# A fused sliding-window attention and feed-forward kernel: w_in in a tile per load, x laid out by token block, attention of chunk 1 two blocks ahead, idle products during the first loads

## The chip, the cores and the metric

The kernel runs on one core of a Trainium2 chip. The metric is the device time of one execution in microseconds (us), from inputs in the chip's HBM to the output there; lower is better. It is compared by the median of several runs. Engines are named as in the profile: PE is TensorE, PEld its weight loads, DVE is VectorE, ACT ScalarE, POOL GpSimd, SP SyncE; SPq, ACTq and POOLq are the queues on which these engines issue DMAs.

## The reference

```python
# q, k, v: (8, 8, 576, 64) float32;  w_in: (512, 2048);  w_out: (2048, 512)
scores = scale * np.matmul(q, k.transpose(0, 1, 3, 2))      # scale = 1/8
rel = pos[:, None] - pos[None, :]
scores = np.where((rel >= 0) & (rel < 64), scores, -1e9)
attn = softmax(scores)
attn_out = np.matmul(attn, v)
x = attn_out.transpose(0, 2, 1, 3).reshape(8 * 576, 8 * 64)
h = x @ w_in
g = h * (1.0 / (1.0 + np.exp(-1.702 * h)))
return g @ w_out                                            # (4608, 512) float32
```

## The kernel before

The 4608 tokens are 36 blocks `m` of 128 tokens and 9 chunks `ch` of 512. A block holds two query groups of 64 tokens; a batch has nine such groups, so a block can lie in two batches.

**Attention of a block** is a chain over four engines. `scores(m)` makes sixteen small products on PE into the one PSUM tile `S`; `exp(m)` reads it on ACT into `E`; `mask(m)` multiplies by a 0/1 mask on DVE into `PT`; `pv(m)` makes sixteen products with v (which carries a column of ones for the row sums) into the one PSUM tile `Tacc`; `norm(m)` divides on DVE (`rc`, `xs`). The block is then turned into `xT`, [512 features in 4 groups of 128, tokens]: for chunks 0 to 3 by `x_mm` on PE and the copy `x_out` on ACT, for later chunks by a transposing DMA from SP (`x_dma`).

**q and k** must be turned as well (`qkt`). Batches 0 and 1 come in three parts of pairs (`load_pairs` on SP, `cast_pairs` to bf16 on two engines, `turn_pairs`: sixteen transposes on PE, and a copy each on DVE and ACT). Batch 2 comes by `load_qk` on SP, `cast_qk` on POOL, `turn_dma` on SP; batches 3 to 7 by casting loads on POOL (`load_bf16`) and `turn_dma`. `cast_v` and `shift_v` run on POOL.

**The feed-forward part**: `up_mm` multiplies w_in by xT (a unit is 16 products of 128 columns for one block, or 4 of 512 columns for a chunk) into `hps`, `up_th` (ACT, tanh) and `up_g` (DVE) make `gT`; `down` multiplies by w_out over 16 steps per chunk into `ops`; `down_out` scales on ACT or DVE and stores. From chunk 2 on, one unit of `up` of chunk ch and one step of `down` of chunk ch-1 make a slot (16 per chunk, the first is slot 32), and tables (`at`, `later`, `slot_pv`) say at which slot attention and loads are issued.

**What sets the order.** Each engine works through its instructions in the order in which the code issues them, and the code writes that order out by hand. Waits between engines are put in by the framework from what each instruction reads and writes of a tile. In the kernel before, w_in is one tile that three loads fill (512, 512 and 1024 of the 2048 columns, issued from POOL behind `gate`, a copy that waits for the last of the first k loads). The rows of xT are [4 feature groups, 512 tokens], so a block is four pieces of a row.

Of the kernel before, what the change touches and what calls it, by code (L numbers as in the profile page):

```python
# [29 lines left out]
def kernel(  # L30
# [94 lines left out]

    def cast_pairs(b, i, engines):
        n = pairs(i)
        for w in range(2):
            copy_on(
                engines[w],  # L130
                out=rows[b % 2][w][0:n, 2 * i : 2 * i + 2, :].rearrange(
                    "p r (h d) -> p h r d", d=D
                ),
                in_=stage_qk[(3 * b + i) % 2][0:n, w, :].rearrange(
                    "p (h r d) -> p h r d", r=2, d=D
                ),
            )

    def turn_pairs(b, i, tiles):
        n = pairs(i)  # L140
        for w in range(2):
            for r in range(2):
                for hp in range(4):
                    nc.tensor.transpose(  # L144
                        out=tiles[w][:, hp, r, 0:n],
                        in_=rows[b % 2][w][0:n, 2 * i + r, P * hp : P * hp + P],
                        identity=ident[0:n, 0:n],
                    )
        for w in range(2):
            copy_on(  # L150
                DA[w],
                out=qkt[b % 2][:, w::2, PAD + 256 * i : PAD + 256 * i + 2 * n].rearrange(
                    "p g (n r) -> p g n r", r=2
                ),
                in_=tiles[w][:, :, :, 0:n].rearrange("p g r n -> p g n r"),
            )
# [267 lines left out]
    norm(1)  # L424
    warm(2)
    x_mm(1, psO, "O")
    scores(2)
    exp(2)
    x_out(1)
    scores(3)  # L430
    exp(3)
# [187 lines left out]
```

## Time and profile before

| | |
|---|---|
| median of 3 runs | 333.69 us (332.8 to 335.26) |
| the profiled execution's own time | 335.44 us |
| its span, first to last instruction | 333.7 us |
| PE busy | 304.0 us (91% of the span), 3226 products |
| PE weight loads busy | 194.9 us (58%) |
| DVE, ACT, POOL busy | 164.6, 156.2 and 136.5 us |
| mean granted clock of PE | 0.984 |

The span is cut by the code into a head (first loads, attention of blocks 0 to 3, `up` of chunk 0, to 44.2 us), `down` of chunk 0 (to 61.2), a stage in which chunk 1's `up` and the attention of blocks 5 to 8 alternate (to 90.9), and the slots. A PE that is busy in the record is not at its peak, so what matters is where it stands idle, who ended each wait, and at which clock it ran.

### The profile page before, as it was taken

Reading aid. Unit: us, or ns where it says so; the run is one execution under the profiler, and the core shown is the slowest. Engines: PE = TensorE matmul, PEld = TensorE weight load, DVE = VectorE, ACT = ScalarE, POOL = GpSimd, SP = SyncE. Lnnn points to the kernel's source line nnn. Section 1 sums busy time; section 2 is a strip of 40 time slices with the busy share of each in tenths; the row PEclk is TensorE's granted clock in tenths of the full one; section 3 lists DMA queues with packets and bytes.
Section 4 is the critical chain, followed back from the end, with each engine's and each line's share of the span. In section 5 each row is a group of like instructions: output and inputs, shape, how many; then the busy total and the mean of one; then the engine's idle time right before and its main releaser. Section 6 shows DMA issues by size and latency. Waiting matters only on the chain.

```text
span 333.7 us, 7775 instructions
## 1 busy us (share of the span) xinstructions
PE 304.0 (91%) x3226; PEld 194.9 (58%) x3226; DVE 164.6 (49%) x276; ACT 156.2 (47%) x240; POOL 136.5 (41%) x196
## 2 busy tenths in 40 slices
PE   1677999778899979999899999999999999999995
PEld 1437545567767757777577777775555544444442
DVE  5352732467655535655455655555545554433400
ACT  2542622655555535564455454555455543444411
POOL 1850465086697869737876537720000000000000
PEclk9995999999999979999999999999999999999999
DMA  8999890599799999999999999994433312000121
GB/s 193 210 210 215 217 256 10 167 215 171 148 96 120 134 155 154 125 160 134 200 141 186 207 109 168 141 117 89 87 82 79 81 47 79 33 31 31 34 94 63
DMA packets 150995, 43.31 MB, mean 130 GB/s; under 512 B 135088, under 2 KB 145328, under 8 KB 150960
## 3 DMA queue, kind: packets, MB, share of 16 engines
q0 software_dynamic: 72480, 13.05, 56.1%
q1 hardware_dynamic: 74448, 22.43, 37.5%
q10 hardware_dynamic: 4032, 7.34, 6.8%
q8 instruction: 25, 0.41, 0.6%
q14 instruction: 10, 0.08, 0.1%
HBM read 36.70 MB, written 9.44 MB: 138 GB/s over the span
## 4 chain that ended last, share of the span: by engine, by line
PE 79%; DMA 9%; ACT 4%; DVE 2%; SPq 2%; POOL 1%; issue 1%; ACTq 0%
PE hps L336 36%; PE ops L366 36%; PE Tacc L280 4%; DMA w_in_sb<-in_moe_w_in_dram 3%; PE S L251 3%; DMA xT_dma<-xs 2%; DMA qkt<-rows_k 2%; DMA stage_qk<-in_k_dram 2%; ACT th L347 2%; ACT xT_pe L319 1%; DVE PT L266 1%; PE turn L144 1%; SPq L85 1%; ACT E L261 1%; SPq L119 1%
## 5 line engine op out<-in xcount | busy, mean ns | idle before, releaser
L353 DVE SCALAR_TENSOR_TENSOR gT<-th,hps 128x512 bf16<-128x512 bf16 x144 | 99.0, 688 | 121.5 <-ACT th L347 121.0
L366 PE MATMUL ops<-w_out_sb,gT 128*128 128x512 bf16 x576 | 144.6, 382 | 0.5 <-DVE gT L353 0.5
L347 ACT ACTIVATE th<-hps 128x512 bf16<-128x512 f32 x144 | 86.0, 597 | 123.7 <-PE hps L336 119.0
L336 PEld LDWEIGHTS <-w_in_sb 128*128 128x128 bf16 x1328 | 109.0, 115 | 47.3 <-issue 6.7
L336 PE MATMUL hps<-xT_dma,w_in_sb 128*128 128x256 bf16 (+1 forms) x448 | 82.5, 318 | 1.4 <-DMA xT_dma<-xs 1.4
L366 PEld LDWEIGHTS <-gT 128*128 128x128 bf16 x576 | 53.0, 98 | 52.5 <-issue 1.4
L336 PE MATMUL hps<-xT_pe,w_in_sb 128*128 128x128 bf16 (+1 forms) x880 | 67.6, 234 | 4.9 <-DMA w_in_sb<-in_moe_w_in_dram 2.6
L261 ACT ACTIVATE E<-S 128x1024 bf16<-128x1024 f32 x36 | 36.7, 1019 | 5.0 <-PE S L251 5.0
L172 POOL DMA_DIRECT2D v_nat<-in_v_dram x25 | 21.4, 854 | 17.5 <-issue 17.3
L380 ACT ACTIVATE o_sb<-ops 128x512 f32<-128x512 f32 x34 | 20.2, 599 | 17.5 <-PE ops L366 17.5
L293 DVE TENSOR_TENSOR xs<-Tacc,rc 128x512 bf16<-128x512 f32 x36 | 24.9, 692 | 1.2
L176 POOL COPY v_off<-v_nat 64x528 bf16<-64x528 bf16 x25 | 16.0, 642 | 18.2 <-DMA v_nat<-in_v_dram 17.5
L266 DVE TENSOR_TENSOR PT<-E,mask_None 128x1024 bf16<-128x1024 bf16 x28 | 21.0, 749 | 2.9 <-ACT E L261 2.9
L251 PE MATMUL S<-qkt 64*128 64x64 bf16 x576 | 15.7, 195 | 7.0 <-ACT qkt L104 2.8
L171 POOL DMA_DIRECT2D rows_k<-in_k_dram x25 | 21.4, 855 | 0.0
L171 POOL DMA_DIRECT2D rows_q<-in_q_dram x25 | 21.2, 847 | 0.0
L251 PEld LDWEIGHTS <-qkt 64*128 64x128 bf16 x576 | 11.0, 97 | 14.1 <-issue 7.3
L280 PE MATMUL Tacc<-v_off,PT 128*64 128x65 bf16 x320 | 16.6, 201 | 0.8 <-DVE PT L266 0.8
L280 PEld LDWEIGHTS <-PT 128*64 128x64 bf16 x576 | 12.6, 114 | 5.3 <-DVE PT L266 3.6
L280 PE MATMUL Tacc<-v_nat,PT 128*64 128x65 bf16 x256 | 14.8, 202 | 0.6 <-DVE PT L266 0.3
L92 POOL CAST v_off<-stage_v 64x512 bf16<-64x512 f32 x15 | 9.6, 639 | 12.0 <-DMA stage_v<-in_v_dram 11.5
L104 ACT COPY qkt<-turn 128x1024 bf16<-128x1024 bf16 (+1 forms) x6 | 4.8, 799 | 18.4 <-DVE qkt L104 15.4
(43 smaller groups left out, 119.5 us busy)
## 6 DMA issues: line engine op xcount, KB each, us to landing
out_dram<-o_sb ACTq DMA_DIRECT2D x28, 256.0 KB, 3.1
stage_v<-in_v_dram SPq DMA_DIRECT2D x12, 256.0 KB, 6.1
rows_q<-in_q_dram POOLq DMA_DIRECT2D x20, 128.0 KB, 5.5
rows_k<-in_k_dram POOLq DMA_DIRECT2D x20, 128.0 KB, 6.2
v_nat<-in_v_dram POOLq DMA_DIRECT2D x20, 128.0 KB, 6.1
stage_qk<-in_q_dram SPq DMA_DIRECT2D x4, 512.0 KB, 5.4
stage_qk<-in_k_dram SPq DMA_DIRECT2D x4, 512.0 KB, 6.1
w_out_sb<-in_moe_w_out_dram POOLq DMA_DIRECT2D x4, 512.0 KB, 12.9
```

The lines of the kernel that those rows point to most:

```text
L171: nc.gpsimd.dma_start(out=heads(rows[b % 2][w][0:n, i, :]), in_=rows_of(src, b, i))
L172: nc.gpsimd.dma_start(out=v_nat[b % 2][0:n, i, :, 0:D], in_=rows_of(v, b, i))
L251: nc.tensor.matmul(st[:, h % 2, t * 256 + hp * 64 : t * 256 + hp * 64 + 64], lhsT=src[part, 2 * hp + 1, 64 * j : 64 * j + 128], rhs=src[pa ...
L261: nc.scalar.activation(out=E_of[m][:], in_=S_of.pop(m)[:], func=AF.Exp, scale=scale)
L266: nc.vector.tensor_tensor(out=pt[:].rearrange("p a f -> p (a f)"), in0=E_of.pop(m)[:].rearrange("p a f -> p (a f)"), in1=masks[z][:].rearr ...
L280: nc.tensor.matmul(acc[t * 64 : t * 64 + 64, h // 4, (h % 4) * 66 : (h % 4) * 66 + 65], lhsT=pt[:, epos : epos + 64], rhs=win, start=True, ...
L293: nc.vector.tensor_tensor(out=xs[:].rearrange("p (b h d) -> p b h d", b=2, h=4), in0=view[:, :, :, 0:D], in1=rc[:].to_broadcast([P, 2, 4, D]),
L336: nc.tensor.matmul(ps[:, g, :], lhsT=w_in_sb[:, c, f0 + (f + g) % 4 : f0 + 512 : 4], rhs=xT[ch][:, c, t0 : t0 + nt], start=(c == 0), stop= ...
L347: nc.scalar.activation(out=th[:], in_=ps[:], func=AF.Tanh, scale=0.851)
L353: nc.vector.scalar_tensor_tensor(out=gT[ch, f // 4][:, f % 4 : f % 4 + nf, t0 : t0 + nt], in0=th[:], scalar=1.0, in1=ps[:], op0=ALU.add, o ...
L366: nc.tensor.matmul(O_of[ch, tsub][:, :], lhsT=gT[ch, j][:, f, tsub * P : (tsub + 1) * P], rhs=w_out_sb[:, 4 * j + f, :], start=(j == 0 and ...
L380: nc.scalar.activation(out=o_sb[:], in_=ps[:], func=AF.Copy, scale=0.5)
```

## The change

Four things change, and parts of the order around them.

1. `w_in_sb` becomes three tiles, one per load; `up_mm` reads the one in which its columns lie.
2. A chunk's `xT` is [4 token blocks, 4 feature groups, 128 tokens], so that a block is one contiguous piece of a row; a product over 256 or 512 tokens now reads two or four pieces of 128 tokens.
3. In the head, idle products (`warm`, now 128 columns wide, both operands from the identity) stand between the steps of attention from the start on, and the casts and turns of q and k are issued one by one.
4. In chunk 1's stage `scores` runs two blocks ahead and `pv` one, `x_mm` comes before the last `up` unit of a block, `cast_pairs(1, 1)` and its turn come before the loop, the loads and casts of batch 2 come one block earlier, and the slots of attention up to block 26 move one slot earlier.

```diff
-    w_in_sb = keep.tile([P, 4, DFF], bf16, name="w_in_sb")
+    w_in_sb = [keep.tile([P, 4, n], bf16, name=f"w_in_sb{i}") for i, n in enumerate((512, 512, 1024))]
...
+    def cast_pair(b, i, w, engine):
...
+    def turn_mm(b, i, w, tiles):
+        n = pairs(i)
+        for r in range(2):
+            for hp in range(4):
+                nc.tensor.transpose(
+                    out=tiles[w][:, hp, r, 0:n],
+                    in_=rows[b % 2][w][0:n, 2 * i + r, P * hp : P * hp + P],
+                    identity=ident[0:n, 0:n],
+                )
+
+    def turn_out(b, i, w, tiles):
+        n = pairs(i)
+        copy_on(
+            DA[w],
...
-            xT[ch] = xt_pool.tile([P, 4, 512], bf16, name=f"xT_{how}", tag=f"xT_{how}")
-        return xT[ch][:, :, (m % 4) * P : (m % 4) * P + P]
+            xT[ch] = xt_pool.tile([P, 4, 4, P], bf16, name=f"xT_{how}", tag=f"xT_{how}")
+        return xT[ch][:, m % 4]
...
-                    lhsT=w_in_sb[:, c, f0 + (f + g) % 4 : f0 + 512 : 4],
-                    rhs=xT[ch][:, c, t0 : t0 + nt],
+                    lhsT=w_in[:, c, f0 + (f + g) % 4 : f0 + 512 : 4],
+                    rhs=xT[ch][:, m0 : m0 + nt // P, c, :],
...
-            nc.tensor.matmul(ps[:, :], lhsT=ident[:], rhs=rhs, start=True, stop=True)
-
-
-    cast_pairs(0, 0, DA)
+            nc.tensor.matmul(ps[:, :], lhsT=ident[:], rhs=ident[:], start=True, stop=True)
...
+    cast_pairs(0, 0, DA)
+    warm(34)
+    tiles = turn_tiles(psH, "H")
+    turn_mm(0, 0, 0, tiles)
+    turn_out(0, 0, 0, tiles)
+    warm(10)
+    turn_mm(0, 0, 1, tiles)
+    turn_out(0, 0, 1, tiles)
+    warm(8)
     scores(0)
     exp(0)
+    cast_pair(0, 1, 0, nc.vector)
+    warm(10)
     scores(1)
     exp(1)
+    cast_pair(0, 1, 1, nc.scalar)
     mask(0)
     pv(0)
-    cast_pairs(0, 1, DA)
     norm(0)
-    warm(2)
+    tiles = turn_tiles(psH, "H")
+    turn_mm(0, 1, 0, tiles)
+    mask(1)
+    turn_out(0, 1, 0, tiles)
+    warm(6)
     x_mm(0, psO, "O")
...
     mask(2)
     pv(2)
     norm(2)
-    warm(3)
+    u = up_mm(0, 0, 4, 0, P, wide=True)
+    u = up_th(*u)
+    mask(3)
     x_mm(2, psO, "O")
     x_out(2)
-    mask(3)
     pv(3)
     norm(3)
-    up(0, 0, 4, 0, P, wide=True)
+    up_g(*u)
     up(0, 0, 4, P, P, wide=True)
+    up(0, 0, 4, 2 * P, P, wide=True)
     x_mm(3, psT, "T")
     x_out(3)
-    up(0, 0, 4, 2 * P, P, wide=True)
     up(0, 0, 4, 3 * P, P, wide=True)
...
     mask(4)
+    scores(5)
     pv(4)
     norm(4)
+    exp(5)
+    cast_pairs(1, 1, (nc.gpsimd, nc.scalar))
     down_out(0, 2)
     down_out(0, 3, on_dve=True)
+    mask(5)
     x_mm(4, psT, "T")
     x_out(4)
-    load_pairs(1, 2)
-    load_v(1, 4)
+    turn_pairs(1, 1, turn_tiles(psT, "T"))
...
         u = up_mm(1, 0, 4, t0, P, wide=True)
-        scores(m + 1)
+        scores(m + 2)
+        pv(m + 1)
         u = up_th(*u)
-        exp(m + 1)
+        exp(m + 2)
         up_g(*u)
...
         norm(m + 1)
-        up_g(*u[1])
+        up(1, 4, 4, t0, P, wide=True)
+        mask(m + 2)
+        up(1, 8, 4, t0, P, wide=True)
...
-        up(1, 12, 4, t0, P, wide=True)
         x_mm(m + 1, psT, "T")
         x_out(m + 1)
+        up(1, 12, 4, t0, P, wide=True)
...
-    slot_pv = {8: 32, 9: 34, 10: 38, 11: 42, 12: 45}
+    slot_pv = {8: 31, 9: 33, 10: 37, 11: 41, 12: 44}
...
-    for i in range(2, 5):
-        at(4 * i + 24, lambda i=i: cast_qk(2, i))
-        at(4 * i + 24, lambda i=i: turn_dma(2, i))
...
+    for i in range(3, 5):
+        at(4 * i + 21, lambda i=i: cast_qk(2, i))
+        at(4 * i + 21, lambda i=i: turn_dma(2, i))
```

What stands in a row on three engines, first before and then after. **PE, at the first unit of `up`** (the first products of the kernel that read w_in; DMASW0, 1 and 2 are the semaphores of the three loads of w_in, and a weight load fetches the w_in columns of the product behind it). Before:

```order
L336 LDWEIGHTS w_in_sb [waits DMASW0_49]
L336 MATMUL hps<-xT_pe,w_in_sb 128x128
L336 LDWEIGHTS w_in_sb [waits DMASW2_49,DMASW1_49]
L336 MATMUL hps<-xT_pe,w_in_sb 128x128
L336 LDWEIGHTS w_in_sb
```

And after, at the same unit:

```order
L349 LDWEIGHTS w_in_sb_112 [waits DMASW0_49]
L349 MATMUL hps<-xT_pe,w_in_sb_112 128x128
L349 LDWEIGHTS w_in_sb_112
L349 MATMUL hps<-xT_pe,w_in_sb_112 128x128
L349 LDWEIGHTS w_in_sb_112
```

The second weight load waited for all three loads of w_in before; after, the unit waits for the first load alone, and the other two waits stand at the first unit that reads their tiles.

**ACT, from `exp(4)` at the end of chunk 0's `down` into chunk 1's stage** (E is exp, o_sb a store's scaling, xT_pe is `x_out`, qkt a copy of a turn, th the tanh of a unit of `up`). Before:

```order
L261 ACTIVATE E<-S 128x1024
L380 ACTIVATE o_sb<-ops 128x512 x2
L319 COPY xT_pe<-pxt 128x4x128
L347 ACTIVATE th<-hps 128x512
L261 ACTIVATE E<-S 128x1024
L347 ACTIVATE th<-hps 128x512 x3
L319 COPY xT_pe<-pxt 128x4x128
L104 COPY qkt_107<-turn 128x4x256
```

And after:

```order
L272 ACTIVATE E<-S 128x1024
L393 ACTIVATE o_sb<-ops 128x512
L272 ACTIVATE E<-S 128x1024
L104 CAST rows_k_105<-stage_qk_93 128x8x2x64
L393 ACTIVATE o_sb<-ops 128x512
L330 COPY xT_pe<-pxt 128x512
L104 COPY qkt_107<-turn 128x4x256
L360 ACTIVATE th<-hps 128x512
L272 ACTIVATE E<-S 128x1024
L360 ACTIVATE th<-hps 128x512 x2
L330 COPY xT_pe<-pxt 128x512
L360 ACTIVATE th<-hps 128x512 x2
```

The copy `x_out(4)` has an exp and a cast more ahead of it; in the loop `x_out` moved from behind the fourth tanh of a block to behind the third.

**SP, around slots 33 to 43** (out_dram is a store, qkt_106 takes batches 0, 2, 4 and 6, qkt_107 the odd ones; a piece of 64 is the fifth and last of its batch). Before:

```order
L382 DMA out_dram<-o_sb 128x512
L183 DMA_TRANSPOSE qkt_106<-rows_q_102 128x4x128
L183 DMA_TRANSPOSE qkt_106<-rows_k_103 128x4x128
L382 DMA out_dram<-o_sb 128x512
L183 DMA_TRANSPOSE qkt_106<-rows_q_102 128x4x64
L183 DMA_TRANSPOSE qkt_106<-rows_k_103 128x4x64
L183 DMA_TRANSPOSE qkt_107<-rows_q_104 128x4x128
L183 DMA_TRANSPOSE qkt_107<-rows_k_105 128x4x128
```

And after:

```order
L193 DMA_TRANSPOSE qkt_106<-rows_q_102 128x4x128
L193 DMA_TRANSPOSE qkt_106<-rows_k_103 128x4x128
L395 DMA out_dram<-o_sb 128x512
L193 DMA_TRANSPOSE qkt_106<-rows_q_102 128x4x64
L193 DMA_TRANSPOSE qkt_106<-rows_k_103 128x4x64
L395 DMA out_dram<-o_sb 128x512
L193 DMA_TRANSPOSE qkt_107<-rows_q_104 128x4x128
L193 DMA_TRANSPOSE qkt_107<-rows_k_105 128x4x128
```

The turns of batch 2's fourth and fifth pieces now stand ahead of the stores that they stood behind, so behind the second store only batch 3's first piece is left.

## Rows read from the trace of the kernel before

**Rows 1.** Busy time by engine, clock, DMA share and GB/s, in three stretches.

```profile
core 0: us, PE busy (x) PEld busy (x) DVE busy (x) ACT busy (x) POOL busy (x), PEclk, DMA share, GB/s
24.40:44.20 19.80, 17.21 (x122) 12.07 (x119) 10.80 (x17) 9.50 (x18) 3.40 (x5) 0.83 1.02 219
61.20:90.90 29.70, 23.09 (x453) 20.32 (x454) 19.79 (x33) 16.86 (x28) 17.33 (x26) 1.00 0.97 194
116.60:130.00 13.40, 11.41 (x165) 8.39 (x164) 5.43 (x9) 5.63 (x10) 9.81 (x13) 0.87 1.91 155
```

**Rows 2.** The chain that ended last: start us, us, what; two of its DMAs.

```profile
16.88 10.22 DMA w_in_sb<-in_moe_w_in_dram
...
115.05 6.49 DMA qkt<-rows_k
```

**Rows 3.** PE in order of time: start us, us, instruction [idle before <-who ended it].

```profile
5.79 1.03 PE L144 MATMUL turn<-ident,rows_q 128*128 128x128 bf16 x8 [5.79 <-DVE rows_q L104]
...
27.23 3.47 PE L336 MATMUL hps<-xT_pe,w_in_sb 128*128 128x128 bf16 x31 [2.59 <-DMA w_in_sb<-in_moe_w_in_dram]
...
61.19 0.45 PE L280 MATMUL Tacc<-v_off,PT 128*64 128x65 bf16 x16
62.70 0.40 PE L314 MATMUL pxt<-ident,xs 128*128 128x128 bf16 x4 [1.06 <-DVE xs L293]
63.77 1.05 PE L336 MATMUL hps<-xT_pe,w_in_sb 128*128 128x128 bf16 x16 [0.67 <-ACT xT_pe L319]
...
69.83 0.61 PE L144 MATMUL turn<-ident,rows_q 128*128 128x128 bf16 x8 [0.72 <-ACT xT_pe L319]
...
73.25 0.29 PE L251 MATMUL S<-qkt 64*128 64x64 bf16 x8 [1.25 <-ACT qkt L104]
...
121.58 0.39 PE L251 MATMUL S<-qkt 64*128 64x64 bf16 x8 [1.99 <-DMA qkt<-rows_k]
...
163.61 1.07 PE L336 MATMUL hps<-xT_dma,w_in_sb 128*128 128x256 bf16 x8 [1.44 <-DMA xT_dma<-xs]
```

**Rows 4.** POOL in order of time: the issue of w_in's first two loads.

```profile
13.28 1.66 POOL L190 DMA_DIRECT2D w_in_sb<-in_moe_w_in_dram  x2
```

**Rows 5.** DMA issues from 13.2 to 13.9 us: KB, us to landing.

```profile
w_in_sb<-in_moe_w_in_dram POOLq DMA_DIRECT2D x1, 512.0 KB, 5.5
```

**Rows 6.** DMA issues from 4.9 to 6.5 us.

```profile
stage_qk<-in_q_dram SPq DMA_DIRECT2D x1, 512.0 KB, 6.1
```

**Rows 7.** SP in order of time.

```profile
4.93 1.63 SPq L119 DMA_DIRECT2D stage_qk<-in_q_dram  x1
...
100.54 0.38 SPq L382 DMA_DIRECT2D out_dram<-o_sb  x1
...
108.85 0.38 SPq L382 DMA_DIRECT2D out_dram<-o_sb  x1
109.33 1.18 SPq L183 DMA_TRANSPOSE qkt<-rows_q  x1
```

**Rows 8.** DVE in order of time, in the head.

```profile
12.62 0.68 DVE L104 CAST rows_q<-stage_qk 128x1024 bf16<-128x1024 f32 x1
...
14.32 0.68 DVE L266 TENSOR_TENSOR PT<-E,mask_None 128x1024 bf16<-128x1024 bf16 x1
16.71 1.23 DVE L104 COPY qkt<-turn 128x1024 bf16<-128x1024 bf16 x1 [1.71 <-PE turn L144]
```

**Rows 9.** ACT in order of time, in the head.

```profile
12.49 1.02 ACT L261 ACTIVATE E<-S 128x1024 bf16<-128x1024 f32 x1 [0.70 <-PE S L251]
...
34.67 0.60 ACT L347 ACTIVATE th<-hps 128x512 bf16<-128x512 f32 x1 [0.27 <-PE hps L336]
...
44.17 0.60 ACT L347 ACTIVATE th<-hps 128x512 bf16<-128x512 f32 x1 [0.27 <-PE hps L336]
```

**Rows 10.** The page's costliest groups: two weight loads (busy, mean ns).

```profile
L336 PEld LDWEIGHTS <-w_in_sb 128*128 128x128 bf16 x1328 | 109.0, 115 | 47.3 <-issue 6.7
L366 PEld LDWEIGHTS <-gT 128*128 128x128 bf16 x576 | 53.0, 98 | 52.5 <-issue 1.4
```

More of the change, by code (lines that the diff above doesn't have):

```diff
@@ L124, in load_pairs @@
             )
+    def cast_pair(b, i, w, engine):
+        n = pairs(i)
+        copy_on(
+            engine,
+            out=rows[b % 2][w][0:n, 2 * i : 2 * i + 2, :].rearrange(
+                "p r (h d) -> p h r d", d=D
+            ),
+            in_=stage_qk[(3 * b + i) % 2][0:n, w, :].rearrange(
+                "p (h r d) -> p h r d", r=2, d=D
+            ),
+        )
     def cast_pairs(b, i, engines):
+        for w in range(2):
+            cast_pair(b, i, w, engines[w])
+    def turn_mm(b, i, w, tiles):
@@ L127, in cast_pairs @@
         n = pairs(i)
-        for w in range(2):
[L129 to L140, printed above, removed]
-        for w in range(2):
[L142 to L156, printed above, removed]
+        for r in range(2):
[4 more added lines that the diff above has]
+                    identity=ident[0:n, 0:n],
+                )
@@ L332, in up_mm @@
         ps = pool.tile([P, nf, nt], fp32, name="hps", tag=tag)
-        f0 = 512 * (f // 4)
+        w_in, f0 = w_in_sb[min(f // 4, 2)], 512 if f >= 12 else 0
+        m0 = t0 // P
         for g in range(nf):
@@ L384, in warm @@
     def warm(n):
-        ps = psO.tile([P, 512], fp32, name="idle", tag="O")
-        rhs = masks[None][:].rearrange("p a t g c -> p (a t g c)")[:, 0:512]
+        ps = psO.tile([P, P], fp32, name="idle", tag="O")
         for _ in range(n):
-            nc.tensor.matmul(ps[:, :], lhsT=ident[:], rhs=rhs, start=True, stop=True)
-    cast_pairs(0, 0, DA)
+            nc.tensor.matmul(ps[:, :], lhsT=ident[:], rhs=ident[:], start=True, stop=True)
     for i in range(2):
@@ L401 @@
         load_w_out(j)
-    nc.gpsimd.tensor_copy(out=stage_qk[0][0:1, 0, 0:1], in_=w_out_sb[0:1, 8, 0:1])
-    turn_pairs(0, 0, turn_tiles(psH, "H"))
+    cast_pairs(0, 0, DA)
[7 more added lines that the diff above has]
+    warm(8)
     scores(0)
     exp(0)
+    cast_pair(0, 1, 0, nc.vector)
+    warm(10)
     scores(1)
     exp(1)
+    cast_pair(0, 1, 1, nc.scalar)
     mask(0)
     pv(0)
-    cast_pairs(0, 1, DA)
     norm(0)
-    warm(2)
+    tiles = turn_tiles(psH, "H")
[3 more added lines that the diff above has]
+    warm(6)
     x_mm(0, psO, "O")
-    mask(1)
+    x_out(0)
     pv(1)
-    x_out(0)
-    turn_pairs(0, 1, turn_tiles(psH, "H"))
+    norm(1)
+    turn_mm(0, 1, 1, tiles)
+    turn_out(0, 1, 1, tiles)
+    warm(8)
+    x_mm(1, psO, "O")
+    scores(2)
+    exp(2)
+    x_out(1)
+    warm(8)
+    scores(3)
+    exp(3)
+    nc.gpsimd.tensor_copy(out=stage_qk[0][0:1, 0, 0:1], in_=w_out_sb[0:1, 8, 0:1])
     load_pairs(0, 2)
@@ L423 @@
     load_v(1, 1)
[L424 to L431, printed above, removed]
-    warm(3)
+    warm(6)
     mask(2)
@@ L531, in later @@
         post.setdefault(slot, []).append(g)
-    slot_pv = {8: 32, 9: 34, 10: 38, 11: 42, 12: 45}
+    slot_pv = {8: 31, 9: 33, 10: 37, 11: 41, 12: 44}
     for m in range(13, NM):
         slot_pv[m] = max(slot_pv[m - 1] + 3, 4 * (m - 4) - 2)
-    for m in range(8, NM):
+    for m in range(9, NM):
         s = slot_pv[m]
@@ L540 @@
             later(s + 2, lambda m=m: mask(m + 1))
-        if m > 8:
-            at(s, lambda m=m: pv(m), [lambda m=m: norm(m)])
-            if m < 16:
-                at(s + 1, lambda m=m: x_mm(m, psT, "T"), [lambda m=m: x_out(m)])
-            else:
-                later(s + 2, lambda m=m: x_dma(m))
-    for i in range(2, 5):
-        at(4 * i + 24, lambda i=i: cast_qk(2, i))
-        at(4 * i + 24, lambda i=i: turn_dma(2, i))
-        at(4 * i + 24, lambda i=i: cast_v(2, i))
-    at(32, lambda: load_qk(2, 4))
-    at(32, lambda: load_v(2, 4))
+        at(s, lambda m=m: pv(m), [lambda m=m: norm(m)])
+        if m < 16:
+            at(s + 1, lambda m=m: x_mm(m, psT, "T"), [lambda m=m: x_out(m)])
+        else:
+            later(s + 2, lambda m=m: x_dma(m))
+    for i in range(3, 5):
+        at(4 * i + 21, lambda i=i: cast_qk(2, i))
+        at(4 * i + 21, lambda i=i: turn_dma(2, i))
+        at(4 * i + 21, lambda i=i: cast_v(2, i))
     for b in range(3, B):
```

55 lines of the change are left out of this document (30 added, 25 removed).

## The prediction

> **What bounds the kernel now.** I read first the busy time by engine, stage by stage: PE is the engine with most work, and behind 130 us it hardly stands idle, so a gain can only come from where it waits or runs at the lower of its two clock levels. [rows 1] give the places: 24.4 to 44.2 us with 2.6 us idle (19.80 - 17.21) and a granted clock of 0.83, chunk 1's stage with 6.6 us idle (29.70 - 23.09), and 116.6 to 130 with 2.0 us idle and a clock of 0.87. Then the chain that ended last, for what sets these places [rows 2], and PE in order of time, for who ended each wait [rows 3].
>
> The head waits for w_in: PE has done the first product of the first unit when it stops for 2.59 us, and the next product starts at 27.23, just behind the landing of the third load at 16.88 + 10.22 = 27.10 [rows 2, 3]. That unit reads only columns of the first load, which was issued at 13.28 and took 5.5 us, so it lay there from 18.8 [rows 4, 5]. The wait is one of the tile's bookkeeping, not of data. Behind it PE runs at the lower level: 0.17 of 19.8 us, 3.4 us worth of the upper level, is missing in that stretch [rows 1]. In chunk 1's stage the waits are of attention: 1.06 us for xs and 0.67 for x_out(4), 0.72 for each of four later x_out (one row stands for 69.83, 78.07, 84.30 and 90.87), 1.25 for the copies of a turn; together 5.9 of the 6.6 us [rows 3]. Later there are two waits for transposing DMAs, 1.99 us at block 13's scores and 1.44 at chunk 4's first unit [rows 3]. From there to the end I see nothing that this change touches.
>
> **The change part by part.**
>
> *Head.* With w_in split, the first unit no longer needs the load of 27.10, and the code puts it before pv(3). What is late next is attention itself, which I follow step by step from the first thing that the change can't move, the landing of q's second part: issued at 4.93, 6.1 us to land, so 11.0 us [rows 6, 7]. Its cast now stands ahead of mask(0) on DVE. Path: cast 0.68, mask(0) 0.68 (12.4), pv(0) 0.45 (12.9), norm(0) 1.06 from pv's end to the turn (13.95), mask(1) 0.68 (14.6), the copy of q's turn 1.23 (15.85), norm(1) about 0.95, turn 0.40 and scores(2) as much (17.6), exp(2) 1.02 (18.7), mask(2) 0.68 (19.4), pv(2) 0.45: the first unit can start at 19.9, behind 18.8, so without a wait for w_in [rows 3, 8, 9]. Then norm(2) 1.06, mask(3) 0.68 and pv(3) 0.45 bring PE to 22.1 with one unit done beside them; two units of 1.05 (24.2), x_mm(3) 0.40; x_out(3) stands behind a tanh of 0.60 and takes about as long (25.5); a last unit, 26.55. Twelve units of 512 columns follow; in the trace eleven of them go by from the tanh at 34.67 to that at 44.17, 0.864 each, so 10.4 us: `up` of chunk 0 ends at 36.9 instead of 44.17 [rows 3, 9]. **Gain 7.2 us.** The eight units that read the third load begin at 30.0, 2.9 us behind its landing, so this DMA stays hidden.
>
> The idle products cost nothing as long as each group ends before its successor's operands come: 34 products of 128 columns at the 0.129 us of eight transposes in 1.03 us take 4.4 us, and the first turn starts at 5.79 today, so they fit if the identity is there by 1.4 [rows 3]; groups of 6 to 10 take 0.8 to 1.3 us beside steps of 1 us on ACT and DVE. If all of them stood in the way by their whole excess, I would lose some 0.5 us. What they may give is the upper clock level early: eight transposes take 1.03 us at 5.79 and 0.61 at 69.83 [rows 3]. My path uses the durations of the upper level; at the lower one its six PE steps cost some 0.2 to 0.4 us more each, 1 to 2 us. I take the upper level, because PE would be busy nearly throughout from the identity on.
>
> *Chunk 0's down.* The same products, 7.2 us earlier. Its loads do not come earlier (SP waits for w_out), but in the trace their casts and turns don't hold PE there, so I cost this at nothing; a load that came late would hold the turn of batch 1's first part, behind the twelfth of the sixteen steps.
>
> *Chunk 1's stage.* Idle before: 6.6 us. What stays: 1.06 for xs(4). At x_out(4) it gets worse: ACT now does exp(5) and a cast, 1.0 each, and a store's 0.6 ahead of it, while only scores(5), 0.4, is new on PE there. From x_mm(4)'s end I count 1.5 us of wait instead of 0.67. The turn of the second pair part, now before the loop, has the same two copies between itself and scores(6) as before, and one unit to hide them: 1.25 stays. The third part's turn, whose copies now stand behind a later tanh and g, costs 0 to 0.7, I take 0.4. The four waits of 0.72 go, three since x_out now has a whole unit (1.05) beside it, and the layout no longer ties blocks of one chunk together. Left: 1.06 + 1.5 + 1.25 + 0.4 = 4.2. **Gain 2.4 us.**
>
> *Slots.* Four slots last 8.31 us between two stores on SP, so a slot is 2.08 [rows 7]. Block 13's scores come one slot earlier, at 119.6 - 2.08 = 117.5 on the old clock. The turn of k that they wait for was issued at 115.05, because from 109.33 on SP had both halves of batch 2's last piece and one half of batch 3's first to issue before it [rows 2, 7]. Two of these are now gone ahead. Then q's half starts at 109.33 and k's at about 110.6, and with the 6.49 us of today it lands at 117.1, 0.4 us before its use. So the 1.99 go, and with them the lower clock behind that wait: 0.13 of 13.4 us, 1.7 at most [rows 1]; part of that stretch is the wait itself, so between 0 and 1.7 I take 1.0. **Gain 3.0 us.** Chunk 4's xT is one slot earlier too, 2.08 against a wait of 1.44: **gain 1.4 us.**
>
> *Layout of x.* A product over 512 tokens now reads four pieces of 128 instead of one. Bounds: nothing, or what a stepped read costs in the nearest row: a weight load from w_in, which takes every fourth element, lasts 115 ns and one from gT, of the same size and contiguous, 98 [rows 10]. 17 ns on each piece of 128 tokens would be the upper bound. There are 240 products of four pieces (12 units of chunk 0 and 48 of chunks 6 to 8, four products each) and 256 of two (chunks 4 and 5), 1472 pieces: 25.0 us. I take nothing, since 127 of 128 reads in a piece stay neighbours, where in the row none are.
>
> The Trainium skill, SBUF — State Buffer, "Door 1", says that reads which hit the same 16-byte line again run at full bandwidth, so a step of up to 8 bf16 elements would be free. By that rule the layout costs nothing and the sum stays as it is; yet by it the two weight loads would be equal too, and here the measured 115 against 98 ns decides that a small step is not free.
>
> **The sum.** 7.2 + 2.4 + 3.0 + 1.4 = 14.0 us. The profiled execution took 335.44 with a span of 333.7; it would take 321.4 with a span of 319.7. The median of the runs shown is 333.69, 1.75 below the profiled one, and I set the forecast against it: **319.7 us**.
>
> **The rivals.**
>
> *SP and the DMAs don't come along.* From the loads of batch 2 on, SP and POOL work without much pause, and the DMA share in the record stands at 1.91 in the last of the three stretches [rows 1]. If this stream follows by the head's 7.2 us alone, and SP's new order brings k's turn no earlier, it lands at 121.5 - 7.2 = 114.3, while PE wants it at 117.5 - 9.6 = 107.9: a wait of 6.4 us, and the lower clock's 1.0 stays. 14.0 - 7.4 = 6.6: 327.1 us. Against it: between 109.33 and 115.05 k's turn stood behind SP's own issues, and two of these now come earlier [rows 2, 7].
>
> *The clock.* The level stays low through the head's attention (1 to 2 us), or falls again before the 512-column units, which costs what is missing today, up to 3.4 us [rows 1]: 321 to 323, say 322.5. For it: the path still has PE waiting about 1 us at a time. Against it: no wait of 2 us is left in the head, and today the level fell behind one of 2.59.
>
> *The layout makes every wide product slower.* At 17 ns a piece it gives 319.7 + 25.0 = 344.7 us, slower than before. It decides from 14.0 / 1472 = 9.5 ns a piece on. For it speaks only the weight load's row; against it, how few steps there are.
>
> *The split frees nothing.* The first unit would still wait to 27.1. The order of the two programs speaks against it, as the semaphores of the second and third load have left the first unit. It would give 330.
>
> **How the numbers follow.** My forecast's case has 0.64, the stream 0.14, the clock 0.14, the layout 0.04, the split and things unseen 0.04. The clock's case lies inside the range anyway. Upwards the range takes in the stream's case, so 327; downwards the 4.2 us that I left idle in chunk 1's stage could in part go as well, so 316. Runs of this kernel spread over 0.7%, so about 1% (3.3 us) is what can be told from no change; faster by over 1% is all but the layout's case and half of the last: 0.93, the same 0.03, slower 0.04.
>
> **What would show it.** In the profile of the changed kernel: the first unit at about 20 us with no wait for w_in; the last tanh of chunk 0 near 37; no x_out wait inside the loop, but a longer one before the turn ahead of it; slot 32 some 9 us earlier than 90.9; block 13's scores without a wait for a DMA, and a clock of 1.00 there; the 256- and 512-column products at the same mean as before. The forecast is wrong if the attention path has a step that I missed on DVE or ACT, if wide products are longer, or if PE, 10 us ahead, meets the loads and turns of batches 2 and 3.

## The result and the profile after

The changed kernel takes 319.24 us, the median of 4 runs (318.37 to 320.18), against 333.25 (331.84 to 335.26) for the kernel before, timed beside it: a ratio of 0.9576, 95% interval 0.9518 to 0.9634, 14.0 us less. The forecast was 319.7. The profiled execution took 318.37 us with a span of 316.6. That is 17.1 below the profiled execution of before, which lay 2.2 above its median, while this one lies 0.9 below its own; so a sum made from the two profiles comes out some 3 us larger than the one of medians.

The busy time by engine of the changed kernel, in the stretches that answer to [rows 1]: the head from the first unit to the last tanh of chunk 0, chunk 1's stage from pv(4) to slot 32, and the slots around block 13's scores.

```profile
core 0: us, PE busy (x) PEld busy (x) DVE busy (x) ACT busy (x) POOL busy (x), PEclk, DMA share, GB/s
15.00:18.00 3.00, 3.00 (x39) 2.57 (x38) 2.05 (x4) 1.60 (x2) 2.83 (x5) 0.50 1.09 174
20.00:37.40 17.40, 16.22 (x159) 10.56 (x159) 12.39 (x21) 10.93 (x19) 1.89 (x5) 1.00 1.02 203
54.50:80.60 26.10, 22.05 (x470) 20.38 (x463) 19.50 (x33) 18.80 (x30) 15.22 (x22) 1.00 0.89 188
105.80:114.70 8.90, 8.58 (x150) 6.80 (x150) 4.97 (x9) 5.31 (x9) 7.05 (x9) 1.00 1.95 159
```

The clock is 1.00 in all three, where [rows 1] show 0.83 and 0.87 in two; in their place there is one short stretch at 0.50, from 15 to 18 us. PE of the changed kernel in order of time, with the waits that are left:

```profile
13.06 0.22 PE L291 MATMUL Tacc<-v_off,PT 128*64 128x65 bf16 x1 [1.48 <-DVE PT L277]
13.44 0.62 PE L146 MATMUL turn<-ident,rows_q 128*128 128x128 bf16 x8
15.75 1.04 PE L146 MATMUL turn<-ident,rows_k 128*128 128x128 bf16 x8
...
20.68 1.08 PE L349 MATMUL hps<-xT_pe,w_in_sb 128*128 128x128 bf16 x16
...
25.93 11.41 PE L349 MATMUL hps<-xT_pe,w_in_sb 128*128 128x128 bf16 x64 [0.94 <-ACT xT_pe L330]
...
56.16 0.40 PE L325 MATMUL pxt<-ident,xs 128*128 128x128 bf16 x4 [1.06 <-DVE xs L304]
57.75 0.61 PE L146 MATMUL turn<-ident,rows_q 128*128 128x128 bf16 x8 [1.19 <-ACT xT_pe L330]
...
61.16 0.29 PE L262 MATMUL S<-qkt 64*128 64x64 bf16 x8 [1.25 <-ACT qkt L104]
...
71.85 0.29 PE L262 MATMUL S<-qkt 64*128 64x64 bf16 x8 [0.32 <-ACT qkt L104]
```

Against [rows 3]: the first unit runs at 20.68 in one piece and waits for no w_in; the four waits of 0.72 for x_out inside the loop are gone; and no product of PE waits for a DMA anywhere. Left in chunk 1's stage are 1.06, 1.19, 1.25 and 0.32, where I had left 1.06, 1.5, 1.25 and 0.4. Of the wide products, the costliest groups of PE by shape show no change (before: 379 and 273 ns, 128x512 and 128x256):

```profile
L349 PE MATMUL hps<-xT_dma,w_in_sb 128*128 128x512 bf16 x192 | 49.3, 379 | 0.0
L349 PE MATMUL hps<-xT_dma,w_in_sb 128*128 128x256 bf16 x256 | 33.2, 273 | 0.0
```

To see where the time came from I compare the starts of the 144 tanhs, one for each unit, in every profile: the first and the last of chunk 0, that of some slots (a slot is a unit of chunks 2 to 8), and the last of all. These are ACT's in the changed kernel, against [rows 9]:

```profile
27.88 0.60 ACT L360 ACTIVATE th<-hps 128x512 bf16<-128x512 f32 x1 [0.27 <-PE hps L349]
...
37.38 0.60 ACT L360 ACTIVATE th<-hps 128x512 bf16<-128x512 f32 x1 [0.27 <-PE hps L349]
```

By how many us each profile is ahead of the profiled execution of before (first row: its times):

| | first | last of chunk 0 | slot 32 | slot 44 | slot 48 | slot 64 | last |
|---|---|---|---|---|---|---|---|
| before, at | 29.03 | 44.17 | 91.97 | 117.66 | 129.38 | 164.71 | 315.07 |
| after | 7.22 | 6.79 | 10.39 | 11.86 | 14.69 | 16.93 | 17.10 |
| before_again | 0.10 | 0.86 | 0.41 | 0.52 | -0.75 | 0.67 | 0.74 |
| one_w_in | -0.05 | -0.50 | 2.28 | 3.75 | 6.54 | 8.79 | 9.00 |
| split_only | 2.87 | 4.54 | 4.41 | 4.39 | 5.73 | 6.40 | 6.40 |
| head_only | 7.07 | 6.64 | 4.86 | 5.17 | 7.21 | 8.46 | 8.46 |
| no_idle | 5.86 | 5.81 | 9.41 | 10.88 | 13.71 | 15.47 | 15.47 |
| old_layout | 6.39 | 5.97 | 9.56 | 11.04 | 13.86 | 16.10 | 16.11 |
| late_slots | 7.09 | 6.66 | 10.26 | 11.03 | 14.68 | 14.66 | 14.66 |
| more_idle | 7.72 | 7.29 | 10.30 | 11.77 | 14.59 | 16.83 | 17.06 |
| tuned | 7.73 | 8.18 | 14.17 | 15.64 | 17.75 | 20.00 | 20.21 |
| apart | 8.18 | 8.64 | 14.73 | 16.21 | 19.03 | 20.03 | 20.03 |

So in the profiles the stretches give 6.8 for the head, 3.6 for chunk 1's stage, 1.5 for slots 32 to 44, 2.8 from slot 44 to 48 and 2.4 behind it. Two borders do not part the same work in both orders. At slot 48 the changed kernel has one block's attention more ahead of the border than the kernel before, since it comes one slot earlier; that block is worth 0.8 us: before_again waited for no DMA between slots 48 and 64 and took 33.9 us for them, the changed kernel 33.1. late_slots, with attention where the kernel before has it, is ahead by 11.03 at slot 44 and by 14.68 at slot 48. So block 13's scores are worth 3.6 and chunk 4's first unit 1.4, with 0.2 behind it. At slot 32 it is scores(9), 0.4 us, which the changed kernel does ahead of the border.

The runs were taken in four batches, and the median of the kernel before was 333.25, 332.47, 331.76 and 332.67 in them. A difference of up to some 1.5 us between kernels of different batches is therefore not settled by the times alone; where one is used below, the rows of the profiles carry it.

### The profile page after: what moved, and what is told of

It is laid out like the page before. It is cut to its first block, busy times and chain, and to the rows that moved or that the text cites. A ratio compares the mean times of both kernels' runs of the same rounds, so it can differ in the third digit from the quotient of the medians.

```text
span 316.6 us, 7896 instructions
## 1 busy us (share of the span) xinstructions
PE 295.0 (93%) x3269; PEld 196.1 (62%) x3306; DVE 164.0 (52%) x276; ACT 157.4 (50%) x241; POOL 136.7 (43%) x195
## 4 chain that ended last, share of the span: by engine, by line
PE 86%; ACT 4%; DVE 3%; issue 2%; DMA 2%; SPq 1%; ACTq 0%
PE ops L379 38%; PE hps L349 38%; PE Tacc L291 4%; PE S L262 4%; DMA stage_qk<-in_q_dram 2%; DVE gT L366 1%; PE turn L146 1%; ACT th L360 1%; ACT xT_pe L330 1%; DVE qkt L104 1%; PE pxt L325 1%; SPq L85 1%; ACT qkt L104 1%; DVE PT L277 1%; DVE xs L304 0%
## 5 line engine op out<-in xcount | busy, mean ns | idle before, releaser
L379 PE MATMUL ops<-w_out_sb,gT 128*128 128x512 bf16 x539 | 136.4, 379 | 5.4 <-issue 4.3
L349 PEld LDWEIGHTS <-w_in_sb 128*128 128x128 bf16 x1328 | 106.1, 113 | 40.9 <-issue 1.4
L349 PE MATMUL hps<-xT_pe,w_in_sb 128*128 128x128 bf16 (+1 forms) x880 | 64.7, 228 | 1.1 <-ACT xT_pe L330 0.9
L186 POOL COPY v_off<-v_nat 64x528 bf16<-64x528 bf16 x25 | 16.1, 646 | 27.9 <-DMA v_nat<-in_v_dram 27.3
L188 POOL COPY v_off<-v_nat 64x528 bf16<-64x528 bf16 x20 | 12.9, 644 | 1.2
```

The source lines that it names most:

```text
L349: nc.tensor.matmul(ps[:, g, :], lhsT=w_in[:, c, f0 + (f + g) % 4 : f0 + 512 : 4], rhs=xT[ch][:, m0 : m0 + nt // P, c, :], start=(c == 0), ...
L379: nc.tensor.matmul(O_of[ch, tsub][:, :], lhsT=gT[ch, j][:, f, tsub * P : (tsub + 1) * P], rhs=w_out_sb[:, 4 * j + f, :], start=(j == 0 and ...
```

## The experiments

**before_again**: the kernel before, unchanged, to see how much of [rows 3] belongs to one execution.

> The kernel before, unchanged, for a second profile. Between the two profiled executions 17.1 us of span are gone, between the medians only 14.0 us. Theory A: the waits for transposing DMAs (1.99 us at block 13's scores, 1.44 us at chunk 4's first unit) and the lower clock behind the first vary from execution to execution, and the profiled one had much of them; this profile then shows another size of them and a span nearer to 331.5 us. Theory B: the waits are fixed by the order, and the difference is spread over the span; then both waits are the same again within 0.3 us.

334.71 us in a single run; the kernel before had a median of 332.47 beside it (329.72 to 336.16, 7 runs). The wait for w_in was 2.08, that for k's turn at block 13 3.1, and no product waited for chunk 4's xT. PE's products waited for these two DMAs 1.99 and 1.44 us in the first profile of before, 3.1 and 0 here, 2.13 and 0.78 in split_only, 1.44 and 0.2 in head_only, 0 and 0 in the changed kernel. A wait of this kind is read from one execution to about 1 us. So the waits vary, as theory A has it, but the span of 333.0 is not near its 331.5: the three waits together are only 0.8 us shorter, 5.2 for 6.0.

**one_w_in**: the changed kernel with w_in in one tile again.

```
+    w_in_sb = keep.tile([P, 4, DFF], bf16, name="w_in_sb")
...
+        w_in, f0 = w_in_sb, 512 * (f // 4)
```

> The changed kernel with w_in as one tile again, all else as changed. Theory A (the split frees the head): the first unit stops after one product until the third load lands at 27.1 us; up of chunk 0 then ends 5 to 6.5 us later, near 43, with the clock at its lower level for some us behind a wait of 6 us; 325 us, 1.8% over the changed kernel. Theory B (the head's gain is that of the idle products and of the new order of attention): the wait is back but most of the gain stays, under 2 us lost, 321.

326.8 us (326.44 to 327.41; ratio to before 0.9856, 0.9798 to 0.9915), 7.6 more than the changed kernel (8.1 by the two profiles): theory A, and more than its 5 to 6.5. PE in order of time, and the stretch of the wait in the view by windows:

```profile
20.81 0.25 PE L349 MATMUL hps<-xT_pe,w_in_sb 128*128 128x128 bf16 x1
27.29 1.76 PE L349 MATMUL hps<-xT_pe,w_in_sb 128*128 128x128 bf16 x15 [6.23 <-DMA w_in_sb<-in_moe_w_in_dram]
```

```profile
24.00:27.00 3.00, 0.00 (x0) 0.00 (x0) 0.00 (x0) 0.00 (x0) 0.00 (x0) 0.50 1.14 218
```

One product of the first unit runs, then PE stands until 27.29, where it stood until 27.23 before. All that the new order of attention wins in the head (PE comes to this unit 3.6 us earlier) is waited away, and the whole head's gain with it: the last tanh of chunk 0 is where it was before.

**split_only**: the kernel before with nothing but the split.

```
+    w_in_sb = [keep.tile([P, 4, n], bf16, name=f"w_in_sb{i}") for i, n in enumerate((512, 512, 1024))]
...
+        w_in, f0 = w_in_sb[min(f // 4, 2)], 512 if f >= 12 else 0
```

> The kernel before with nothing changed but w_in, which lies in a tile per load. Theory A (the split itself frees the first unit; the earlier place of the unit in the code and the shorter attention path ahead of it give the rest of the head): the wait of 2.59 us for w_in is gone, since the first load lies there from 18.8 us and the second product was ready at 24.5; what comes back of the lower clock behind it adds 0 to 3.4 us, so a gain of 2.6 to 4.5 us, 329 to 331 us, and the last tanh of chunk 0 at 40 to 41.5 us instead of 44.2. Theory B (the split is the whole of the head's gain, the new order of attention only fills time): 6 to 7 us, 326.5 us, last tanh of chunk 0 near 37.5. Theory C (the product waits for the third load by something other than the shared tile): no change, 333 us.

327.83 us (327.58 to 329.92; ratio 0.9897, 0.9862 to 0.9932), 3.9 less than before: theory A by the gain, with the last tanh of chunk 0 at 39.6 us, a little ahead of its 40. That is 4.5 earlier, which is the wait of 2.59 and 1.9 us of the lower clock behind it. The other 2.3 us of the head need the new order as well, and the order alone is worth nothing there (one_w_in). At block 13 PE waits as before, but with the clock at 1.00 behind it:

```profile
117.34 0.29 PE L252 MATMUL S<-qkt 64*128 64x64 bf16 x8 [2.13 <-DMA qkt<-rows_k]
```

**head_only**: the changed kernel up to the end of chunk 0's `up`, the kernel before from there on (the code of both, cut at the loop over chunk 0's down).

> The changed kernel up to the end of chunk 0's first product, and the kernel before from chunk 0's second product on: its order of chunk 1's attention (one block ahead), of the slots and of SP's loads. Theory A (my terms add up): the head's 6.8 to 7.2 us are kept to the end, and the others, which the two profiles show as 10 us behind the head and the medians as some 7, are not: 326 to 327 us, with waits for xs, x_out and the turn's copies in chunk 1's stage and for a DMA at block 13's scores as before, or longer, since PE gets there 7 us earlier than SP's loads. Theory B (the stream of loads sets the time behind the head): the gain is lost at block 13, 329 to 332 us. Theory C (attention two blocks ahead is worth little, the waits of the stage only moved): 321 to 323 us.

325.82 us (323.8 to 327.01; ratio 0.9796, 0.975 to 0.9842), 5.9 less than before: theory A. Its PE in order of time has the old waits of chunk 1's stage (0.67, 0.72, 1.24 and so on), and at block 13:

```profile
64.49 0.61 PE L146 MATMUL turn<-ident,rows_q 128*128 128x128 bf16 x8 [0.72 <-ACT xT_pe L330]
67.91 0.29 PE L262 MATMUL S<-qkt 64*128 64x64 bf16 x8 [1.24 <-ACT qkt L104]
...
115.86 0.29 PE L262 MATMUL S<-qkt 64*128 64x64 bf16 x8 [1.44 <-DMA qkt<-rows_k]
```

PE came there some 5 us earlier and waited 1.44 us, not longer than before: SP's loads moved along with PE. In the profiled execution, the longest of its four, the granted clock was 0.95 in chunk 1's stage (58.5 to 87.1), in which 1.8 of the head's 6.6 were lost again. By medians the order behind the head is worth 325.82 - 319.24 = 6.6 us (7.3 by the two ratios), where my terms gave 6.8.

**no_idle**: the changed kernel without its idle products (`warm` returns at once).

> The changed kernel without any idle product. Theory A (the first unit is bound by the landing of q's second part and by steps on DVE and ACT, to which PE's clock adds little): the lower level holds through the head's attention, the first unit starts 1 to 1.5 us later than at 20.7, and the total loses 1 to 2 us: 320 to 321. Theory B (the idle products carry the clock into the 512-column units): the units of chunk 0 start at the lower level, as before, and another 2 us or more go: 322 to 324.

320.46 us (319.67 to 321.14; ratio 0.9667, 0.9594 to 0.9739), 1.2 more than the changed kernel: theory A. Turns and scores of the head last 1.03 and 0.61, where they last 0.62 and 0.41 behind idle products; the first unit starts at 21.24 instead of 20.68 and lasts 1.90 instead of 1.08. The next two units, from 23.77 on, last 1.98 together, as they do in the changed kernel: the units behind the first do not need the idle products.

**old_layout**: the changed kernel with x by feature block again.

```
+            xT[ch] = xt_pool.tile([P, 4, 512], bf16, name=f"xT_{how}", tag=f"xT_{how}")
+        return xT[ch][:, :, (m % 4) * P : (m % 4) * P + P]
...
+                    rhs=xT[ch][:, c, t0 : t0 + nt],
```

> The changed kernel with xT as [4 feature groups, 512 tokens] again. Theory A (the layout neither costs nor frees anything; order alone took the waits for x_out out of chunk 1's stage): same time within 0.3%, the same mean of the 256- and 512-column products, no wait for x_out between blocks. Theory B (the old layout ties blocks together): a unit that reads one block waits for the copy of the next, 0.7 us in each of four blocks, 2 to 3 us slower, 322.

319.26 us (317.81 to 319.38; ratio 0.9617, 0.9557 to 0.9677): no difference from 319.24. Its profile is 0.8 us behind the changed kernel's from the first unit on and by the same amount at slot 64; that is the head's clock, which was 0.50 from 13 to 19 us here. No wait for x_out comes back in the loop. So theory A: the layout costs nothing and frees nothing.

**late_slots**: attention's slots 8 to 12 where the kernel before has them.

```
+    slot_pv = {8: 32, 9: 34, 10: 38, 11: 42, 12: 45}
```

> The changed kernel with attention's slots 8 to 12 back at 32, 34, 38, 42, 45, where the kernel before has them; its loads, its order in chunk 1's stage and all else stay as changed. Between the tanhs of slots 32 and 44 the kernel before takes 25.7 us and the changed one 24.2, of which only the 0.41 us of scores(9) was moved out; the rest, 8.31 against 8.07 us for four slots, has no wait behind it in the waits' view. Theory A (it is the place of the slots in the group of four): four slots take 8.3 us again and the sum is 0.7 to 1.0 us slower, 320.2 us. Theory B (it is the load on queues and engines of the loads' old order): 8.07 us as in the changed kernel, 319.2 us. For block 13's scores, one slot later: the wait for k's turn stays away by either, since k's turn came 0.2 us behind its weights' turn before and now has 2 us more.

320.53 us (319.9 to 321.72; ratio 0.9639, 0.9575 to 0.9702), 1.3 more: theory A. ACT's tanhs of slots 36, 40 and 44 stand 8.30 and 8.31 apart again, against 8.07 and 8.08 in the changed kernel:

```profile
90.02 0.60 ACT L360 ACTIVATE th<-hps 128x512 bf16<-128x512 f32 x1 [0.53 <-PE hps L349]
...
98.32 0.60 ACT L360 ACTIVATE th<-hps 128x512 bf16<-128x512 f32 x1 [0.52 <-PE hps L349]
...
106.63 0.60 ACT L360 ACTIVATE th<-hps 128x512 bf16<-128x512 f32 x1 [0.52 <-PE hps L349]
```

What makes four slots 0.24 us longer is x_out. The unit of slot 40 reads block 10, and with attention one slot later x_out(10) stands right ahead of it. In late_slots the unit's first product starts 0.05 us behind the end of that copy (96.60 + 0.58 = 97.18):

```profile
96.60 0.58 ACT L330 COPY xT_pe<-pxt 128x512 bf16<-128x512 bf16 x1
97.23 1.05 PE L349 MATMUL hps<-xT_pe,w_in_sb 128*128 128x128 bf16 x16
```

In the changed kernel the copy ends 1.57 us ahead of the unit:

```profile
94.48 0.58 ACT L330 COPY xT_pe<-pxt 128x512 bf16<-128x512 bf16 x1
96.63 1.06 PE L349 MATMUL hps<-xT_pe,w_in_sb 128*128 128x128 bf16 x16
```

The unit starts 1.10 us behind the start of the `down` step ahead of it in late_slots and 0.86 in the changed kernel, which is the 0.24. The view shows no wait, because the record has PE busy with that step until 97.16. At block 13 there is no wait; at chunk 4's first unit, a slot later for its transposing DMA too, the old one is back:

```profile
148.95 1.06 PE L349 MATMUL hps<-xT_dma,w_in_sb 128*128 128x256 bf16 x8 [1.47 <-DMA xT_dma<-xs]
```

**more_idle, tuned**: idle products in the gap that lowers the clock; then also three waits moved.

```
     exp(1)
     cast_pair(0, 1, 1, nc.scalar)
+    warm(22)
```

```
+    x_mm(3, psT, "T")
+    x_out(3)
     up(0, 0, 4, 2 * P, P, wide=True)
...
     x_out(4)
+    down_out(0, 2)
+    turn_pairs(1, 1, turn_tiles(psO, "O"))
```

> The changed kernel with a group of 22 more idle products behind the second scores and ahead of pv(0), where PE stands idle from 11.6 to 13.1 us and after which the granted clock shows 0.50 from 15 to 18 us. They work out nothing that is used. Theory A (the idle time took the clock): the turn of k takes 0.62 us instead of 1.04 and the first unit of products starts 0.7 to 1.0 us earlier, 318.3 us against 319.2. Theory B (the path is bound by DVE's and ACT's steps there, and PE's level only fills gaps): within 0.3 us of the changed kernel. Against both: the 22 products may reach into pv(0) and cost up to 0.5 us.

318.41 us (317.86 to 320.7; ratio 0.9606, 0.9563 to 0.9649). The turn of k lasts 0.62, and the first unit starts at 20.19:

```profile
11.57 1.40 PE L400 MATMUL idle<-ident 128*128 128x128 bf16 x22
...
15.58 0.62 PE L146 MATMUL turn<-ident,rows_k 128*128 128x128 bf16 x8
```

So the idle time did take the clock: theory A in the mechanism, but only 0.5 us of its 0.7 to 1.0 reached the path. By slot 32 the profile has given that back to the lower clock, which came in chunk 1's stage here (0.88 from 54 to 68 us, 1.00 in the changed kernel), behind the same two waits of 1.06 and 1.19. The unit there takes 1.91 us, in the changed kernel 1.06 (at 58.64):

```profile
57.25 0.61 PE L146 MATMUL turn<-ident,rows_q 128*128 128x128 bf16 x8 [1.19 <-ACT xT_pe L330]
...
58.22 1.91 PE L349 MATMUL hps<-xT_pe,w_in_sb 128*128 128x128 bf16 x16
```

By time it can't be told from the changed kernel.

> The kernel with the added idle group, and three moves at the places where the changed kernel's PE still waits: x_mm(3) and x_out(3) ahead of the third unit of chunk 0 (wait of 0.94 us for x_out), x_out(4) ahead of the third chunk-0 output on ACT (wait of 1.19 us), and the turn of batch 1's second part in two tiles of another pool, so that its two copies need not follow each other's turn (wait of 1.25 us). Theory A (these waits are on the path, and nothing is late right behind them): 0.8 + 0.8 + 1.0 + 0.9 less some 0.5, so 3 us, 316 us. Theory B (what waits next takes half of each): 317.5 us. Theory C (the moved store and copies hold up something else): 319 us or more.

315.2 us (314.32 to 316.01; ratio 0.9496, 0.9468 to 0.9523), 4 less than the changed kernel: theory A, and more than its 3. The waits of 0.94 and 1.19 are gone; the one of 1.25 is 0.21.

**apart**: tuned, with two casts of v moved from POOL to ACT.

```
+    cast_v(0, 0)
+    cast_v(0, 1, (0,))
...
     cast_pair(0, 1, 1, nc.scalar)
+    cast_v(0, 1, (1, 2), nc.scalar)
+    warm(14)
```

> The kernel tuned with two of the three casts of v's second block moved from POOL, where they run at 10.84 and 11.52 us beside DVE's cast of q and mask(0), to ACT, behind its cast of k at 13.9 us; the group of idle products ahead of pv(0) is 14 long instead of 22. Theory A (DVE and POOL hold each other up where both work on SBUF at once; the cast of 0.99 and the mask of 1.09 us are 0.68 each when POOL is still): both take 0.68 us, the first unit starts 0.6 to 0.7 us earlier, 314.5 us against tuned's 315.2, and the cast of v on POOL that took 0.85 us takes 0.61. Theory B (these DVE steps are long for another reason, as the first load of the mask or the clock): 0.99 and 1.09 stay, and the time is tuned's or, with two casts more on ACT ahead of x_out(0), up to 0.5 us slower.

314.8 us (313.94 to 315.57; ratio 0.9464, 0.9422 to 0.9507): not to be told from tuned by time. DVE in the changed kernel, then in this one:

```profile
11.01 0.99 DVE L104 CAST rows_q<-stage_qk 128x1024 bf16<-128x1024 f32 x1 [3.41 <-DMA stage_qk<-in_q_dram]
11.92 1.09 DVE L277 TENSOR_TENSOR PT<-E,mask 128x1024 bf16<-128x1024 bf16 x1
```

```profile
11.07 0.69 DVE L107 CAST rows_q<-stage_qk 128x1024 bf16<-128x1024 f32 x1 [3.40 <-DMA stage_qk<-in_q_dram]
11.68 0.69 DVE L280 TENSOR_TENSOR PT<-E,mask 128x1024 bf16<-128x1024 bf16 x1
```

Theory A holds for the mechanism: in tuned, with the old casts, they still take 0.97 and 1.09; with POOL still, both are back at 0.69, and the first tanh is 0.45 earlier, a little less than its 0.6 to 0.7. The gain is kept up to slot 44 and grows at slot 48, but is gone at slot 64, where this execution waited 1.27 us for chunk 4's xT.

## Why the prediction was right, step by step

**Head, 7.2 forecast, 6.8 measured.** The mechanism was right: the wait was one of the tile (one_w_in, split_only), and what is late next is attention. The last tanh of chunk 0 came at 37.38 instead of 36.9. The first unit was 0.8 us later than my path had it, at 20.68, for two steps that I priced from undisturbed rows: the cast and mask(0), 0.68 each, took 0.99 and 1.09 beside POOL's casts; and the clock, which I took at the upper level throughout, was 0.50 from 15 to 18 us, because DVE's two long steps left PE idle for 1.48 us; filling that idle time (more_idle) brings the first unit 0.5 us forward. I said that the level fell behind a wait of 2.59 and that no wait of 2 us is left; the first half of the clock's rival came true at 1.48, for 3 us. Afterwards the path won back 0.3: x_out(3) held PE 0.94.

**Idle products, nothing forecast.** Right that they stand in nobody's way, and the 1 to 2 us named for the lower level are 1.2 (no_idle).

**Chunk 0's down, nothing forecast.** No wait for its loads appeared.

**Chunk 1's stage, 2.4 forecast, 3.6 measured.** Idle time in the stage fell from 6.6 [rows 1] to 26.10 - 22.05 = 4.05, against the 4.2 that I left, so the waits were sized well: they give 2.6. The other 1.0 is PE counted less busy in the stage, and most of it belongs to the waits as well. First the rows of the kernel before, then those of the changed kernel:

```profile
68.71 0.40 PE L314 MATMUL pxt<-ident,xs 128*128 128x128 bf16 x4
69.83 0.61 PE L144 MATMUL turn<-ident,rows_q 128*128 128x128 bf16 x8 [0.72 <-ACT xT_pe L319]
```

```profile
79.17 0.39 PE L325 MATMUL pxt<-ident,xs 128*128 128x128 bf16 x4
79.39 2.15 PE L349 MATMUL hps<-xT_pe,w_in_sb 128*128 128x128 bf16 x32
```

The next product starts 1.12 us behind x_mm's start before and 0.22 in the changed kernel. So a wait shown as 0.72 cost 0.90, and the four of them 0.7 more than I took. That is the step that I had too small: I priced a wait by the idle time shown, while x_mm's 0.40 of busy time holds PE only for 0.22 where nothing waits. The remaining 0.3 I don't split further.

**Slots 32 to 44, nothing forecast, 1.5 measured.** This term was missing. 0.7 of it is x_out, which held up the first unit of slots 36, 40 and 44 by 0.24 each before and in late_slots; 0.4 is scores(9), which moved into the stage; the last 0.4 is for the most part pv(9), which stood 0.25 us at 96.48 for mask(9) before, and whose mask the changed kernel has done in the stage.

**Block 13's scores, 3.0 forecast, 3.6 measured with the border set right.** SP of the changed kernel in order of time, against [rows 7]:

```profile
97.46 0.35 SPq L395 DMA_DIRECT2D out_dram<-o_sb  x1
97.92 1.22 SPq L193 DMA_TRANSPOSE qkt<-rows_q  x1
99.25 1.21 SPq L193 DMA_TRANSPOSE qkt<-rows_k  x1
```

k's turn is the second behind the store instead of the fourth, and it landed 5.0 us later, 1.4 ahead of its use at 105.69 (forecast: 0.4). The wait went in all kernels with the new SP order but tuned, which still waited 0.5; it went in late_slots too, where the scores stand in their old slot, so it is SP's order that took it. Of the 3.6, 2.0 is the wait as shown and 0.2 what a wait costs beyond that. The lower clock behind it was sized at 1.0: with a wait 0.14 longer and the clock at 1.00, split_only takes 10.4 us from slot 44 to 48, before 11.7, so it was 1.5. It need not come with the wait, as split_only shows.

**Chunk 4's xT, 1.4 forecast, 1.4 measured with the border set right.** Late_slots, a slot later, has the wait again. But the size belongs to executions: 1.44, 0, 0.78, 0.2 in four executions with the old slots, 0.6 on average, and 1.27 in apart with the new ones. That the two profiles show 1.4 is luck in part.

**Layout, nothing taken, bounds to 25 us.** Right: 379 and 273 ns as before, and old_layout takes the same time. The prediction also gave the layout a share in the end of the waits for x_out, as it no longer ties blocks together; that is wrong, since old_layout has none of the four waits either. The slower weight load stays (113 ns for w_in's stepped columns, 98 for gT). That the step costs this, as the prediction has it, is not shown: no run reads w_in without a step, and the weight loads of PT in the changed kernel, which have none, take 111 for 64 columns. For the pieces, the rule of the Trainium skill, SBUF — State Buffer, "Door 1", agrees with the measurement; for the weight load that stays open.

**The rivals.** The stream did not lag: head_only, with SP's old order and PE 5 us early, waited 1.44 us and not 6.4. The split freed the head. The layout made no product slower.

**The sum.** In the two profiles the terms come to 17.1 us, 3.1 over my 14.0: head -0.4, stage +1.2, slots +1.5, block 13 +0.6, chunk 4 and behind +0.2. By medians the change is worth 14.0. The difference is the two profiled executions, of which the one before lay high; setting the sum against the median was right. But how much of the terms' excess is real the runs don't settle, so that the forecast came within 0.5 us of the median is luck in part: the stage and the slots gave 2.7 more than their terms, while the terms were sized on an execution 2.2 above the median.

## What to carry to other kernels

When a tile is filled by several loads and read with a step, look in the chain of waits for a product that starts behind the last load instead of its own; one tile per load is a small edit, but it pays in full only together with an order that lets the freed product come early (3.9 us alone, 7.6 on top of the new order). Price a step from a row in which the neighbouring engines do what they will do after the change, since a cast of 0.68 us was 0.99 beside another engine's casts, and the pause that this made cost the clock as well. Read a wait for a DMA from two executions before it becomes a term of a sum. And where two orders are compared by the time at a border, make sure that the same work lies ahead of it in both.

## What the runs showed of the hardware

DVE and POOL held each other up where both worked on SBUF. POOL in order of time in the changed kernel, beside the two DVE rows shown under apart:

```profile
10.84 0.61 POOL L93 CAST v_nat<-stage_v 128x512 bf16<-128x512 f32 x1
11.52 0.95 POOL L95 CAST v_off<-stage_v 64x512 bf16<-64x512 f32 x1
```

DVE's cast begins at 11.01 and ends 0.55 behind POOL's first one (11.45); POOL's second takes until 0.47 behind DVE's cast (12.00); and mask(0) until 0.54 behind POOL's second (12.47). It looks as though each step's work begins only when the other engine's has ended. The rule of the Trainium skill, SBUF — State Buffer, "Who interferes with whom", says that DVE, in its two-port modes or with two inputs in SBUF, shares a port pair with POOL, and that whoever comes second waits for the whole instruction. The trace agrees.

PE's clock fell behind an idle time of 1.48 us here, and did not where 22 idle products filled most of it (more_idle, 1.00 from 14 to 18 us). The length of one wait does not tell whether it falls. At block 13 it fell behind 1.99 us (before) and held behind 2.13 (split_only); in chunk 1's stage it held behind the waits of 1.06 and 1.19 in the changed kernel and fell behind the same two in more_idle. In the head of no_idle, turns last 1.03 us, as at 0.50, though the column shows 1.00: there the durations tell the level and the column does not.

A wait of PE costs more than the idle time shown, by 0.2 us in three places: 0.90 for 0.72 at x_out in the stage, and from the tanh of slot 45 to the next 4.89 us in split_only and 4.19 in head_only, with waits of 2.13 and 1.44, against 2.58 in late_slots with none. A wait shorter than that does not appear as one, as at slot 40 of late_slots.
